# The first batch of a fused windowed attention and two-layer MLP: two single-bank tiles for layer one's first group, a vector subtraction in the first strided part, identity products on TensorE, and later turns of batch one's plain heads

## The chip, the cores and the metric

The kernel runs on one core of a Trainium2 chip. The metric is device time in microseconds (us). The engines are TensorE (PE, with its weight loads as PEld), VectorE (DVE), ScalarE (ACT), GpSimd (POOL, which here issues the loads) and SyncE (SP, which issues the stores).

## The reference

Eight batches, eight heads, 576 positions, head width 64. Heads 0 to 3 ("plain", z = 0 in the kernel) look back over 32 neighbouring positions; heads 4 to 7 ("strided", z = 1) over 32 positions that are four apart. The result is transposed to 4608 tokens of 512 features and goes through a two-layer MLP with a SiLU between.

```python
scores = scale * np.matmul(q, k.transpose(0, 1, 3, 2))
mask_plain = (rel >= 0) & (rel < window)
mask_dil = (rel >= 0) & (rel < window * dilation) & (rel % dilation == 0)
scores = np.where(masks[None, :, :, :], scores, -1000000000.0)
scores = scores - np.max(scores, axis=-1, keepdims=True)
attn = np.exp(scores)
attn = attn / (np.sum(attn, axis=-1, keepdims=True) + 1e-09)
...
h = x @ w_in                      # 4608x512 by 512x2048
g = h * (1.0 / (1.0 + np.exp(-h)))
return (g @ w_out)                # 2048x512
```

## The kernel before

Each batch goes through the same stages. `transpose` turns q and k on TensorE into head-width-major form; VectorE and ScalarE each copy half of the result out of PSUM. `scores` multiplies blocks of 32 queries with 64 keys. The row maximum is taken (`nm`, negated), the exponential follows on ScalarE (`exps`), `normal` divides by the row sum, `turned` transposes the 32x32 blocks on VectorE (`pt`), `products` multiplies with v into the PSUM tiles `x`, and `finish` copies these into `xT`. `layer1` multiplies `w_in` with `xT` into the PSUM tile `h` (SiLU on ScalarE, into `gT`), and `layer2` multiplies `gT` with `w_out` into `o`, which VectorE copies to `ob` and SyncE stores.

The schedule is written by hand: every engine works through its instructions in the order in which the program issues them. `plan_of(b)` lists, for each batch, at which unit of the MLP an attention stage of the following batches is issued. A unit is one 128-row block of layer one (units 0 to 15) or a quarter of an output tile of layer two (from 16). Batch 0 has no batch in front of it to hide its attention. So its scores are cut in two parts (`scores0`, part 0 for the first 256 positions and part 1 for the other 320), its layer one in the same two parts (`layer1_part`), and the second parts' products are issued at units -8 and -4, that is before rows 8 and 12 of layer one's first part.

PSUM has two pools: `big` with two slots of two banks each, and `ps` with four slots of one bank each. A slot is taken up again when everything that reads its former tile is done. `big` holds, in turn, the four score tiles of batch 0 (strided part 0, plain part 0, strided part 1, plain part 1) and then the `h` groups of layer one; in its first part a group is four rows of 128 by 256 columns. Only the group of rows 8 to 11 lies in two `ps` tiles.

In batch 0 there are two ways from scores to exponentials. `scaled` multiplies the negated maximum by the scale, and ScalarE then takes the exponential of each 64-wide block straight from PSUM, eight to twelve instructions with a bias and a running sum each; the score slot is held until the last of them. `shift0` adds the negated maximum on VectorE and writes the difference to SBUF; this frees the score slot, ScalarE needs a single instruction, and the row sum is then taken by a VectorE reduction in `normal`. Before the change only plain part 1 takes the second way:

```python
scores0(1, 0); scaled(1, 0)        # strided, part 0
transpose(0, 0, 1, both); transpose(0, 0, 0, both)
exps(0, 1, 0)
scores0(0, 0); scaled(0, 0); exps(0, 0, 0)
turn0(1, 0)                        # normal + turned
scores0(1, 1); scaled(1, 1); values0(1, 0); finish0(1, 0, (act, act))
exps(0, 1, 1); turn0(0, 0)
scores0(0, 1); values0(0, 0); finish0(0, 0)
shift0(0, 1); exps(0, 0, 1)
```

Lines in the profile are those of the kernel before: L243 transposes, L266 and L279 plain and strided scores, L321 the mask's product, L338 maximum, L348 `shift0`, L354 `scaled`, L418 the exponential in one instruction, L429 the exponentials by block, L438 row sum, L442 to L445 `normal`, L457 `turned`, L482 products with v, L541/L546 `finish0`, L578 `layer1_part`, L598 layer two of batch 0, L554 layer one of the later batches, L607/L608 copy and store of the output.

Of the kernel before, what the change touches and what calls it, by code (L numbers as in the profile page):

```python
# [9 lines left out]
F32 = mybir.dt.float32  # L10
# [5 lines left out]
P = 128  # L16
# [11 lines left out]
def kernel(  # L28
# [275 lines left out]
    def scores0(z, part):  # L304

        n = (2, 3)[part]
        w = width(0, z, part)
        sd = big.tile([P, 16, KB], F32, tag="big", name=f"s0_{z}_{part}")
        if z:
            sd = sd.rearrange("p (m t) c -> p m t c", m=2)  # L310
            if part:
                parts = [(sd[:, m, 0 : 2 * n], mask_b[:, 1:2].broadcast_to([W, 2 * n, KB])) for m in (0, 1)]
            else:
                pair = mask_b.rearrange("p t c -> p (t c)")[:, None, :].broadcast_to([W, 2, 2 * KB])
                parts = [(sd[:, m, 0:4].rearrange("p (e t) c -> p e (t c)", e=2), pair) for m in (0, 1)]
        elif part:
            parts = [(sd[:, o : o + x], mask_b[:, 1:2].broadcast_to([W, x, KB])) for o, x in ((0, 8), (8, 2))]
        else:
            parts = [(sd[:, 0], mask_b[:, 0]), (sd[:, 1:8], mask_b[:, 1:2].broadcast_to([W, 7, KB]))]
        for i, (t, x) in enumerate(parts):  # L320
            nc.tensor.matmul(  # L321
                t, ident4.rearrange("p h q -> p (h q)"), x,
                start=bool(z or part or i == 0), stop=True, skip_group_check=not (z or part),
            )
# [10 lines left out]
        nm = stat.tile([P, WM], F32, tag="nm", name=f"nm_0_{z}_{part}")  # L335
        raw = sd[:, :, 0 : 2 * n] if z else sd[:, 0:w]
        d = nm[:, 0:w].rearrange("p (m t) -> p m t", m=2) if z else nm[:, 0:w]
        nc.vector.tensor_reduce(out=d, in_=raw, axis=AX.X, op=ALU.max, negate=True)  # L338
        a = att(0)
        a["raw", z, part], a["nm", z, part] = raw, nm  # L340

    def shift0(z, part):

        a = att(0)
        w = width(0, z, part)
        ms = a["ms", z, part] = msp.tile([P, WM, KB], F32, tag="ms", name=f"ms_0_{z}_{part}")
        nm = a["nm", z, part][:, 0:w, None].broadcast_to([P, w, KB])
        nc.vector.tensor_tensor(ms[:, 0:w], a["raw", z, part], nm, ALU.add)  # L348
        a["shifted", z, part] = True

    def scaled(z, part):
# [59 lines left out]
    def exps(b, z, hi):  # L411
# [16 lines left out]
        for t in range(w):  # L428
# [2 lines left out]
                bias=a["nm", z, hi][:, t : t + 1], scale=k, accum_out=l[:, t : t + 1],  # L431
            )

    def normal(b, z, hi):
        a = att(b)
        w = width(b, z, hi)
        if ("shifted", z, hi) in a:
            nc.vector.tensor_reduce(  # L438
                out=a["l", z, hi][:, 0:w], in_=a["pe", z, hi][:, 0:w], axis=AX.X, op=ALU.add
            )  # L440
        r = stat.tile([P, WM], F32, tag="r", name=f"r_{b}_{z}_{hi}")
        nc.vector.tensor_scalar(r[:, 0:w], a["l", z, hi][:, 0:w], EPS, None, ALU.add)  # L442
        nc.vector.reciprocal(r[:, 0:w], r[:, 0:w])
        pn = a["pn", z, hi] = pp_.tile([P, WM, KB], F16, tag="pn", name=f"pn_{b}_{z}_{hi}")
        nc.vector.tensor_tensor(  # L445
            pn[:, 0:w], a["pe", z, hi][:, 0:w], r[:, 0:w, None].broadcast_to([P, w, KB]), ALU.mult
        )
# [70 lines left out]
                        x.rearrange("d (r i) -> d r i", r=2)[:, :, 0:CL],  # L518
                    )

    def values0(z, part):


        a = att(0)
        a["opened"] = set()
        n = (8, 10)[part] if z == 0 else (2, 3)[part]
        j0 = part * (2 if z else 8)
        x = a["x", z] = [
            ps.tile([P, WM * QB], F32, tag="ps", name=f"x_0_{z}_{part}_{hp}") for hp in (0, 1)
        ]  # L530
        for c in range(DIL if z else 1):
            products(0, z, part, c, j0, j0 + n, lambda j: (0, x, (c * n + j - j0) * QB))

# [32 lines left out]
    def layer1_part(f, part):  # L566

        xT = state[0]["xT"]
        c0, c1 = ((0, SA), (SA, S))[part]
        n, w = ((4, SA), (2, 512))[part]  # L570
        if part == 0 and f == 8:
            hs = [ps.tile([P, 2, w], F32, tag="ps", name=f"h_0_{f}_{part}_{x}") for x in (0, 1)]
        else:
            hs = [big.tile([P, n, w], F32, tag="big", name=f"h_0_{f}_{part}")]
        m = n // len(hs)
        for i in range(n):
            for c in range(MC):
                nc.tensor.matmul(  # L578
                    hs[i // m][:, i % m, 0 : c1 - c0],
                    w_in16[:, c, (f + i) * P : (f + i + 1) * P],  # L580
                    xT[:, c, c0:c1],
                    start=(c == 0),
                    stop=(c == MC - 1),
                )
# [60 lines left out]
    def plan_of(b):  # L645
        ev = {}

        def at(s, fn, *args):
            ev.setdefault(s, []).append((fn, args))

        def all_exps(b, z):
            for hi in (0, 1):
                at(16, exps, b, z, hi)

        if b == 0:

            at(-8, values0, 1, 1)
            at(-8, finish0, 1, 1, (act, act))
            at(-4, values0, 0, 1)
            at(-4, finish0, 0, 1)  # L660
            at(-4, build_mask)
            at(1, load_qk, 2)
            transposes(at, 1, 1, 2)
            at(6, scores, 1, 1)
            for hi in (0, 1):
                at(6, shift, 1, 1, hi)
            transposes(at, 1, 0, 10)
            at(14, scores, 1, 0)
            at(14, shift, 1, 0, 1)
            at(15, load_qk, 3)  # L670
            at(15, load_v, 2)
            all_exps(1, 1)
            for hi in (0, 1):
                at(20, exps, 1, 0, hi)
            later(at, 1, 1, (18, 19, 24, 25), act)
            later(at, 1, 0, (23, 24, 28, 29), act)
        elif b == 1:
            at(16, load_v, 3)
            transposes(at, 2, 0, 3)
            transposes(at, 2, 1, 10)  # L680
            transposes(at, 3, 0, 17, (dve, dve))
            at(8, scores, 2, 0)
            at(17, load_qk, 4)
            at(13, scores, 2, 1)
            all_exps(2, 0)
            all_exps(2, 1)
            at(20, scores, 3, 0)
            at(21, exps, 3, 0, 0)
            at(21, exps, 3, 0, 1)
            later(at, 2, 0, (22, 24, 27, 28))  # L690
            later(at, 2, 1, (29, 31, 33, 34))
        else:
            if b + 2 < B:
                at(16, load_v, b + 2)
            if b + 1 < B:
                if b == 2:
                    for n in (0, 1):
                        at(1 + 2 * n, transpose, 3, 1, 1 - n, both)
                later(at, b + 1, 0, (0, 0, 4, 6))
                if b + 3 < B:  # L700
                    at(16, load_qk, b + 3)
            if b + 2 < B:
                transposes(at, b + 2, 0, 13)
                at(17, scores, b + 2, 0)
# [12 lines left out]

        return plan
# [8 lines left out]
    build_mask_b()  # L727
    transpose(0, 1, 0, both)
    scores0(1, 0)
    scaled(1, 0)  # L730
    transpose(0, 0, 1, both)
    transpose(0, 0, 0, both)
    exps(0, 1, 0)
    scores0(0, 0)
    scaled(0, 0)
    exps(0, 0, 0)
    turn0(1, 0)
    scores0(1, 1)
# [62 lines left out]
```

## Time and profile before

| | us |
|---|---|
| median of 3 runs | 321.7 (321.03 to 323.43) |
| the profiled execution | 321.21 |
| its span | 319.4 |
| TensorE busy | 300.5 (94%) |
| ScalarE busy | 216.3 (68%) |
| VectorE busy | 192.5 (60%) |
| start of the first layer-one product | 21.51 |
| start of layer two of batch 0 | 45.28 |

The span runs from the first to the last instruction of the program; the 1.8 us beside it lie around the span. Busy shares are averages over stages that have different limits: TensorE is nearly idle for much of the first 21 us and nearly without a gap after it.

### The profile page before, as it was taken

How to read it: one execution, taken by the hardware profiler on the slowest of the kernel's cores; microseconds unless marked ns; L12 is line 12 of the kernel's file. 1: busy time of each engine (PE TensorE's matmuls, PEld its weight loads, DVE VectorE, ACT ScalarE, POOL GpSimd, SP SyncE). 2: the span in 40 equal slices, each digit the busy share in tenths (PEclk: the TensorE clock that was granted, in tenths of full speed). 3: DMA queues.
4: the chain of work that ended last, by engine and by line, in shares of the span. 5: the costliest groups of instructions: out<-in, count | busy, mean ns of one | idle time of the engine just before them, and what ended most of it. 6: DMA issues, size and time to landing. Idle time of an engine off the chain costs nothing.

```text
span 319.4 us, 11506 instructions
## 1 busy us (share of the span) xinstructions
PE 300.5 (94%) x5040; PEld 192.9 (60%) x5040; DVE 192.5 (60%) x360; ACT 216.3 (68%) x715; POOL 75.6 (24%) x127
## 2 busy tenths in 40 slices
PE   2669989999999999999999999999999999999995
PEld 2348644577545776467745776467745676467544
DVE  2695679616799855893587555893588542740011
ACT  2786756565999658985799458986699457726300
POOL 8825275724002800090005400060000000000000
PEclk9999999999999999999999999999999999999999
DMA  7999999995412960198016930190001100110021
GB/s 117 175 207 205 207 137 201 196 136 78 76 69 70 155 107 2 72 152 141 2 65 91 179 65 4 66 141 8 4 35 68 66 4 3 66 68 0 2 98 66
DMA packets 42081, 28.77 MB, mean 90 GB/s; under 512 B 20928, under 2 KB 37552, under 8 KB 42032
## 3 DMA queue, kind: packets, MB, share of 16 engines
q0 software_dynamic: 36704, 18.61, 44.7%
q1 hardware_dynamic: 5328, 9.44, 8.1%
q8 instruction: 39, 0.64, 0.9%
q14 instruction: 10, 0.08, 0.1%
HBM read 37.21 MB, written 9.44 MB: 146 GB/s over the span
## 4 chain that ended last, share of the span: by engine, by line
PE 80%; DVE 7%; ACT 5%; DMA 4%; issue 2%; POOL 1%; POOLq 0%; DVEq 0%
PE h L554 35%; PE o L622 30%; PE h L578 5%; PE x L482 4%; PE t L243 3%; ACT pe L429 3%; DMA n<-in_q_dram 2%; DVE pn L445 2%; DVE pt L457 2%; DMA w_in<-in_moe_w_in_dram 2%; PE s L279 1%; PE s L266 1%; DMA out_dram<-ob 1%; DVE ob L607 1%; DVE ms L297 1%
## 5 line engine op out<-in xcount | busy, mean ns | idle before, releaser
L554 PE MATMUL h<-xT,w_in 128*128 128x288 f16 x896 | 115.0, 287 | 0.2 <-DVE ob L607 0.2
L622 PE MATMUL o<-w_out,gT 128*128 128x512 f16 (+1 forms) x528 | 114.6, 373 | 0.0
L562 ACT ACTIVATE gT<-h 128x576 f16<-128x576 f32 x112 | 72.8, 650 | 59.0 <-PE h L554 58.1
L554 PEld LDWEIGHTS <-w_in 128*128 128x128 f16 x896 | 85.9, 98 | 24.1 <-issue 0.7
L622 PEld LDWEIGHTS <-gT 128*128 128x128 f16 x528 | 50.2, 98 | 54.4
L429 ACT ACTIVATE pe<-ms,nm 128x64 f32<-128x64 f32 x236 | 78.3, 334 | 0.1
L607 DVE COPY ob<-o 128x512 f32<-128x512 f32 (+1 forms) x37 | 24.8, 671 | 46.4 <-PE o L622 44.0
L429 ACT ACTIVATION_READ_ACCUMULATOR pe<-ms,nm 128x1 f32 x236 | 44.4, 188 | 0.0
L125 POOL DMA_DIRECT2D vw<-in_v_dram x32 | 18.4, 582 | 106.8 <-PE x L482 102.8
L297 DVE SCALAR_TENSOR_TENSOR ms<-s,mask 128x512 f32<-128x512 f32 x28 | 19.2, 686 | 40.3 <-PE s L279 21.6
L457 DVE STREAM_TRANSPOSE pt<-pn 128x640 f16<-128x640 f16 (+2 forms) x32 | 26.0, 812 | 1.1
L445 DVE TENSOR_TENSOR pn<-pe,r 128x640 f16<-128x640 f32 (+2 forms) x32 | 25.3, 792 | 1.1
L134 POOL DMA_DIRECT2D vw<-in_v_dram x32 | 21.2, 670 | 11.3 <-DMA w_out<-in_moe_w_out_dram 5.7
L359 DVE TENSOR_REDUCE nm<-ms 128x10 f32<-128x640 f32 (+1 forms) x28 | 22.0, 787 | 1.0
L578 PE MATMUL h<-xT,w_in 128*128 128x256 f16 (+1 forms) x128 | 18.4, 301 | 3.8 <-ACT pe L429 2.0
L482 PEld LDWEIGHTS <-vw 32*64 32x64 f16 (+1 forms) x1264 | 13.4, 107 | 8.8 <-issue 7.2
L482 PE MATMUL x<-pt,vw 32*64 32x64 f16 (+2 forms) x1264 | 15.5, 193 | 2.7 <-DVE pt L457 1.2
L578 PEld LDWEIGHTS <-w_in 128*128 128x128 f16 x128 | 12.6, 103 | 7.7 <-issue 4.2
L586 ACT ACTIVATE gT<-h 128x640 f16<-128x640 f32 (+2 forms) x13 | 9.9, 767 | 9.6 <-PE h L578 9.4
L516 DVE CAST xT<-x 128x288 f16<-128x288 f32 x24 | 16.3, 823 | 0.0
L243 PEld LDWEIGHTS <-n 64*64 64x64 f16 (+1 forms) x912 | 10.9, 105 | 6.0 <-issue 5.3
L598 PE MATMUL o<-w_out,gT 128*128 128x512 f16 x64 | 14.5, 380 | 0.0
(67 smaller groups left out, 223.4 us busy)
## 6 DMA issues: line engine op xcount, KB each, us to landing
out_dram<-ob SPq DMA_DIRECT2D x35, 256.0 KB, 2.0
n<-in_k_dram POOLq DMA_DIRECT2D x9, 288.0 KB, 5.6
n<-in_q_dram POOLq DMA_DIRECT2D x9, 288.0 KB, 6.4
vw<-in_v_dram POOLq DMA_DIRECT2D x31, 80.0 KB, 4.2
vw<-in_v_dram POOLq DMA_DIRECT2D x32, 72.0 KB, 4.0
w_in<-in_moe_w_in_dram POOLq DMA_DIRECT2D x4, 512.0 KB, 9.2
w_out<-in_moe_w_out_dram POOLq DMA_DIRECT2D x4, 512.0 KB, 11.3
n<-in_k_dram POOLq DMA_DIRECT2D x14, 144.0 KB, 7.3
```

The source lines that it names most:

```text
L134: nc.gpsimd.dma_start(out=vw[h * QB : h * QB + QB, 0:NB], in_=v[b, h].rearrange("(m p) d -> p m d", p=QB))
L297: nc.vector.scalar_tensor_tensor(out=out, in0=in0, scalar=scale, in1=in1, op0=ALU.mult, op1=ALU.add)
L359: nc.vector.tensor_reduce(out=nm[:, 0:w], in_=ms[:, 0:w], axis=AX.X, op=ALU.max, negate=True)
L429: nc.scalar.activation(pe[:, t, :], src[t], AF.Exp, bias=a["nm", z, hi][:, t : t + 1], scale=k, accum_out=l[:, t : t + 1],)
L445: nc.vector.tensor_tensor(pn[:, 0:w], a["pe", z, hi][:, 0:w], r[:, 0:w, None].broadcast_to([P, w, KB]), ALU.mult)
L457: nc.vector.transpose(a["pt"][key][:, o : o + w].rearrange("p t c -> p (t c)"), a["pn", z, hi][:, 0:w].rearrange("p t c -> p (t c)"),)
L482: nc.tensor.matmul(x[h // 2][h % 2 * D : h % 2 * D + D, col : col + wd], vws[b % 2][r, NB + kb * DIL + c if z else kb], pt[r, at : at + wd ...
L554: nc.tensor.matmul(h[:, half, 0:HS], w_in16[:, c, f * P : f * P + P], xT[:, c, half * HS : half * HS + HS], start=(c == 0), stop=(c == MC ...
L562: nc.scalar.activation(gT[:, f, s0 : s0 + S].rearrange("p (a c) -> p a c", a=2), h[:, :, 0:HS], AF.Silu)
L578: nc.tensor.matmul(hs[i // m][:, i % m, 0 : c1 - c0], w_in16[:, c, (f + i) * P : (f + i + 1) * P], xT[:, c, c0:c1], start=(c == 0), stop=( ...
L607: copy(ob, o)
L622: nc.tensor.matmul(o[:, 0, 0:m], gT[:, f, t * P : (t + 1) * P], w_out16[:, f, cols], start=(f == 0), stop=(f == NFF - 1),)
```

## The change

Four edits, all in the work of batch 0 and in the plan that is laid beside it:

- Strided part 0 of batch 0 takes the way of `shift0` in place of `scaled`. Its exponential is one instruction, issued ahead of ScalarE's copy of the plain q; its row sum (`total`) is issued on VectorE behind the two plain copies.
- `warm` issues products of the identity with itself, 256 columns each: three ahead of the products of strided part 0 (into the tile that these then overwrite), four ahead of those of plain part 0, and four ahead of layer one's first group.
- Layer one's first group of the first part (rows 0 to 3) lies in two `ps` tiles, with a SiLU each; the group of rows 8 to 11 lies in `big` with one SiLU.
- In batch 0's plan the transposes of batch 1's plain heads are issued at unit 12 (before 10), and their scores and the shift of their second half at unit 17 (before 14). Unit 17 lies behind the first four products of layer two. What is issued from unit 18 on stays.

```diff
+        nm = att(0)["nm", z, part] = stat.tile([P, WM], F32, tag="nm", name=f"nm_0_{z}_{part}")
...
-        nm = a["nm", z, part][:, 0:w, None].broadcast_to([P, w, KB])
-        nc.vector.tensor_tensor(ms[:, 0:w], a["raw", z, part], nm, ALU.add)
+        nm, o = a["nm", z, part][:, 0:w], ms[:, 0:w]
+        if z:
+            o = o.rearrange("p (m t) c -> p m t c", m=2)
+            nm = nm.rearrange("p (m t) -> p m t", m=2)[:, :, :, None].broadcast_to([P, 2, w // 2, KB])
+        else:
+            nm = nm[:, :, None].broadcast_to([P, w, KB])
+        nc.vector.tensor_tensor(o, a["raw", z, part], nm, ALU.add)
...
+    def total(b, z, hi):
+        a = att(b)
+        w = width(b, z, hi)
+        nc.vector.tensor_reduce(
+            out=a["l", z, hi][:, 0:w], in_=a["pe", z, hi][:, 0:w], axis=AX.X, op=ALU.add
+        )
+        a["summed", z, hi] = True
...
+    def warm(t, n):
+
+        for _ in range(n):
+            nc.tensor.matmul(
+                t[:, 0:SA], ident, ident[:, None, :].broadcast_to([P, SA // P, P]),
+                start=True, stop=True, skip_group_check=True,
+            )
...
+        warm(x[0], idle)          # values0, ahead of its products
...
-        if part == 0 and f == 8:
+        if part == 0 and f == 0:
             hs = [ps.tile([P, 2, w], F32, tag="ps", name=f"h_0_{f}_{part}_{x}") for x in (0, 1)]
+            warm(hs[0].rearrange("p n w -> p (n w)"), 4)
...
-            transposes(at, 1, 0, 10)
-            at(14, scores, 1, 0)
-            at(14, shift, 1, 0, 1)
+            transposes(at, 1, 0, 12)
+            at(17, scores, 1, 0)
+            at(17, shift, 1, 0, 1)
...
     scores0(1, 0)
-    scaled(1, 0)
+    shift0(1, 0)
     transpose(0, 0, 1, both)
+    exps(0, 1, 0)
     transpose(0, 0, 0, both)
-    exps(0, 1, 0)
+    total(0, 1, 0)
     scores0(0, 0)
...
-    values0(1, 0)
+    values0(1, 0, 3)
...
-    values0(0, 0)
+    values0(0, 0, 4)
```

Against the kernel before, TensorE has eleven more products with their weight loads ahead of layer one; VectorE has one instruction more; ScalarE has the exponential of strided part 0 once in place of eight times, and copies batch 1's plain k and q behind the SiLU of rows 10 and 11 and no longer ahead of it.

More of the change, by code (lines that the diff above doesn't have):

```diff
@@ L334, in scores0 @@
                     score(0, h, 8 * part + j, sd[:, j], False)
-        nm = stat.tile([P, WM], F32, tag="nm", name=f"nm_0_{z}_{part}")
+        nm = att(0)["nm", z, part] = stat.tile([P, WM], F32, tag="nm", name=f"nm_0_{z}_{part}")
         raw = sd[:, :, 0 : 2 * n] if z else sd[:, 0:w]
@@ L339, in scores0 @@
         a = att(0)
-        a["raw", z, part], a["nm", z, part] = raw, nm
+        a["raw", z, part] = raw
     def shift0(z, part):
@@ L436, in normal @@
         w = width(b, z, hi)
[L437 to L440, printed above, removed]
+        if ("shifted", z, hi) in a and ("summed", z, hi) not in a:
+            total(b, z, hi)
         r = stat.tile([P, WM], F32, tag="r", name=f"r_{b}_{z}_{hi}")
@@ L519, in finish, with values0 @@
                     )
-    def values0(z, part):
+    def warm(t, n):
[4 more added lines that the diff above has]
+            )
+    def values0(z, part, idle=0):
         a = att(0)
```

## The prediction

> **What bounds the kernel now.** I read the page's totals first, then what TensorE waits for, then the first 30 us in order of time.
>
> ```profile
> span 319.4 us, 11506 instructions
> PE 300.5 (94%) x5040; PEld 192.9 (60%) x5040; DVE 192.5 (60%) x360; ACT 216.3 (68%) x715; POOL 75.6 (24%) x127
> PE t L227 <- DMA n<-in_k_dram: 5.5, 1, 5.5
> PE h L578 <- ACT pe L429: 2.0, 1, 2.0
> PE h L578 <- issue: 1.8, 1, 1.8
> PE t L243 <- issue: 0.6, 1, 0.6
> ```
>
> TensorE is busy for all but 18.9 us, and 5.5 of these are the first load. Of its other waits the longest ends with ScalarE's exponentials by block (L429), which hold the score slots; the next is put down to "issue", which no semaphore explains. So time won ahead of layer one shows in the end, if no later wait takes it back. The change works on the stretch that follows (the timeline: start, duration, engine, line):
>
> ```profile
> 9.23 0.69 DVE L338 TENSOR_REDUCE nm<-s 128x8 f32<-128x512 f32 x1 [0.90 <-PE s L279]
> 10.03 0.75 DVE L247 COPY kT<-t 128x576 f16<-128x576 f16 x1
> 11.02 0.76 DVE L247 COPY qT<-t 128x576 f16<-128x576 f16 x1 [0.23 <-PE t L243]
> 11.59 0.32 ACT L429 ACTIVATE pe<-s,nm 128x64 f32<-128x64 f32 x1
> 11.83 0.61 PE L266 MATMUL s<-kT,qT 64*32 64x64 f16 x32 [0.31 <-DVE qT L247]
> 12.50 0.69 DVE L338 TENSOR_REDUCE nm<-s 128x8 f32<-128x512 f32 x1 [0.72 <-PE s L266]
> 13.92 0.36 ACT L429 ACTIVATE pe<-s,nm 128x64 f32<-128x64 f32 x1
> 14.12 0.80 PE L321 MATMUL s<-mask_b,ident 32*128 32x384 bf16 x2 [1.68 <-ACT pe L429]
> 15.27 0.71 DVE L457 STREAM_TRANSPOSE pt<-pn 128x512 f16<-128x512 f16 x1
> 16.13 0.61 PE L482 MATMUL x<-pt,vw 32*64 32x64 f16 x32 [0.67 <-DMA w_in<-in_moe_w_in_dram]
> 16.67 0.71 PE L321 MATMUL s<-mask_b,ident 32*128 32x512 bf16 x2
> 16.78 1.29 ACT L541 CAST xT<-x 128x256 f16<-128x256 f32 x2 [0.34 <-PE x L482]
> 18.10 0.71 DVE L457 STREAM_TRANSPOSE pt<-pn 128x512 f16<-128x512 f16 x1
> 18.87 0.61 PE L482 MATMUL x<-pt,vw 32*64 32x64 f16 x32 [0.83 <-DVE pt L457]
> 19.52 0.76 DVE L546 CAST xT<-x 128x256 f16<-128x256 f32 x2
> 21.27 0.81 ACT L418 ACTIVATE pe<-ms 128x640 f32<-128x640 f32 x1
> 21.51 4.98 PE L578 MATMUL h<-xT,w_in 128*128 128x256 f16 x32 [2.02 <-ACT pe L429]
> 25.98 0.84 DVE L457 STREAM_TRANSPOSE pt<-pn 128x640 f16<-128x640 f16 x1
> 27.04 1.92 PE L578 MATMUL h<-xT,w_in 128*128 128x256 f16 x16
> 28.89 0.70 PE L482 MATMUL x<-pt,vw 32*64 32x32 f16 x44
> ```
>
> The reader sees two things at 21.51. Both halves of plain xT have been there since 20.28, yet layer one waits for ScalarE's twelve exponentials, whose slot its group takes. And its first 32 products take 4.98 us where 16 of the same form take 1.92 later: TensorE starts slowly. The windows view shows how far (a stretch, then TensorE's busy time and count in it):
>
> ```profile
> 21.60:24.20 2.60, 2.60 (x13) 1.84 (x13) 1.00 1.23 208
> ```
>
> Up to 24.2 a product comes each 0.2 us (0.21, since one of the 13 began earlier). The 16 at 27.04 come each 0.11, with the last one's own length at their end, and 13 of 0.21 and 19 of 0.11 make the 4.98. So the clock doubled near 24.2, though the granted clock in that row (1.00) does not show it.
>
> **Strided part 0.** Removed: eight exponentials, 2.33 us of ScalarE (11.59 to 13.92), and a scaling of 0.17 on VectorE. Added: one exponential of 128x512, which I take at 0.65 (0.81 is the row for 640 columns; by width it would be 0.65), a subtraction of 0.69 and a reduction of 0.69 on VectorE (512 columns, as L338's). The subtraction runs from 9.95 to 10.64 in front of the plain copies: kT goes from 10.03 to 10.56, qT from 11.02 to 11.24, for it waited 0.23 on TensorE before. Plain scores so start at 12.05 and no longer at 11.83, the maximum at 12.72 (the reduction for the sum ends at 12.6, just ahead), and ScalarE starts on the plain exponentials at 13.70 instead of 13.92. Of 2.33 us saved on ScalarE the path gets 0.2, since the work behind it comes later.
>
> What gains more is VectorE: the strided turn waits for no accumulator. Its transpose ends at 15.40, not 15.98, and the strided products run at 15.55, not 16.13. Strided part 1's scores, in a slot that is free at 10.64, run at 12.55, not 14.12. These scores end by 14.0. The next ones need the plain exponentials' slot, free near 16.2 (13.70 and eight blocks of 0.29, with the last sum's read-out), so they start at 16.28 for 16.67. ScalarE's copies start at 16.26 for 16.78; the twelve exponentials behind them, whose end lets TensorE go at 21.51 now, end as much earlier, near 20.95. The plain transpose ends at 18.23 for 18.81, its products start at 18.36 for 18.87, VectorE's copies at 19.03 for 19.52.
>
> **Identity products.** Each takes 0.21 us while slow. Three fit between 13.9 and 15.55. Four from 17.45 end at 18.30, when the plain transpose is ready. Four from 18.8 end at 19.62, while the xT copies run. All are covered; without that cover the last two groups would cost 0.85 us each.
>
> **Two single banks.** The `ps` tiles are free when ScalarE's copies end, at 17.55. Layer one starts as soon as xT is there, at 19.65, the second product at 19.85: 1.8 us earlier. Its second group takes the slot that the exponentials free at 20.95, reached later than that. The plain second part of attention takes up the two `ps` tiles, so it needs their SiLUs. These stand right behind the exponential that now begins at 21.27, and have until 26.4. The extra SiLU costs ScalarE a start, under the 0.65 of a whole such instruction, in that same slack.
>
> **The clock.** It doubled 2.7 us after the first layer-one product. In the changed kernel TensorE is occupied nearly without a gap from 16.3 on, with full-size products from 17.45. If it again takes some 2.7 to 3.4 us of those, the clock comes at 20.2 to 20.9; if the identity products did nothing, at about 24.2 as now. I take 20.9. The Trainium skill ("TensorE: Matmul & The Clock Gate", Part 1) has free-running windows of 3.4 us; by them the clock would come at 24.2 - 3.4 = 20.8, or a window later. The trace agrees with the doubling.
>
> With 20.9, 32 products from 19.65 end near 23.7 (26.4 now), and the strided second part (under 0.7, as its plain sister at 28.89) and 16 more products (1.8) near 26.1. There VectorE takes over: its last transpose, now until 26.83, follows the twelve exponentials and ends at 26.31, so the plain second part runs at 26.40 for 28.89. **Head: 2.5 us.** With the clock at 24.2 it would be 1.1.
>
> **Units 12 and 17.** Now the rows behind it:
>
> ```profile
> 38.47 0.83 PE L243 MATMUL t<-ident,n 64*64 64x64 f16 x72
> 39.23 0.44 PE L578 MATMUL h<-xT,w_in 128*128 128x320 f16 x2
> 41.47 2.07 PE L578 MATMUL h<-xT,w_in 128*128 128x320 f16 x14 [1.80 <-issue]
> 43.47 0.70 PE L266 MATMUL s<-kT,qT 64*32 64x64 f16 x64
> 45.28 8.02 PE L598 MATMUL o<-w_out,gT 128*128 128x512 f16 x36
> 53.23 0.34 PE L482 MATMUL x<-pt,vw 32*64 32x64 f16 x20
> 54.23 0.71 PE L482 MATMUL x<-pt,vw 32*64 32x64 f16 x60 [0.67 <-DVE r L442]
> 48.26 0.82 DVE L438 TENSOR_REDUCE l<-pe 128x10 f32<-128x640 f32 x1 [0.37 <-ACT pe L418]
> 62.68 0.69 DVE L607 COPY ob<-o 128x512 f32<-128x512 f32 x1 [0.62 <-DMA out_dram<-ob]
> q8 instruction: 39, 0.64, 0.9%
> q8 instruction: 1, 0.02, 2.7%
> 35.75:39.50 3.75, 3.75 (x139) 2.71 (x137) 3.23 (x6) 2.13 (x4) 0.66 (x1) 1.00 1.25 209
> 41.40:83.60 42.20, 40.67 (x767) 26.16 (x768) 27.25 (x47) 27.18 (x53) 21.51 (x35) 1.00 1.07 149
> ```
>
> The wait at 39.5 I read as one for code. The queue for instructions moves 39 blocks for TensorE's 10080 instructions, 258 each; one of them moves between 39.2 and 41.4 (second q8 line, the DMA view of that stretch). Between the two "issue" waits lie 767 products and 768 loads, six times 256: both stand at a block's start. So a block begins two products behind the transposes. The block before it began 256 instructions earlier, near 35.75, inside batch 1's strided scores (the window to 39.50 counts 276 with those in flight at its start). If crossing that border asks for the next block, it was at hand 5.7 us later, at 41.47. The 22 added instructions move the borders back, the second one into the transposes, and one more group of eight products (1.09, at 0.136 each by the row at 41.47) stands in between. TensorE needs the block 3.75 + 1.09 - 0.35 = 4.5 us after it asks: the wait falls from 1.96 to 1.2 us, **0.75 gained**. Bounds: none left, or as long as before. The Trainium skill ("Runtime: NRT & Kernel Launch", Instruction fetch mechanics) calls such a crossing mostly hidden; these rows disagree, and by it the wait would be gone, the first rival below.
>
> The move puts two things ahead of batch 1's plain scores: the group of rows 14 and 15 (1.09) and four products of layer two (0.88, a ninth of the 8.02 for 36), 1.97 us. They start at 43.47 - 2.5 - 0.75 + 1.97 = 42.2. This matters, because from these scores to the strided products of unit 24 the chain of waits lies on VectorE without a pause (43.47 to 54.23, but for 0.37 on ScalarE, which is early now). So the products' second part starts at 42.2 + 10.76 - 0.37 = 52.6, for 54.23: 1.63 earlier. TensorE is there at 50.0 (42.2 and 9.76, as from 43.47 to 53.23, less the 1.97 of work that now lies ahead) and stands 2.3 us, some of it behind the 20 products that are ready, instead of 0.7: half of what was won ends here. From there both chains keep their distance. The stores of batch 0 start earlier into loads that keep their time; the fourth copy waits for the first store (0.62). I take 0.2 lost, from 0 (the store takes as long as now) to 1.6 (it lands when it does now).
>
> **Sum.** 2.5 + 0.75 - 1.97 + 0.37 - 0.2 = 1.45 us off the profiled 321.21: **319.8**, which is 1.9 under the median of 321.7.
>
> **Rivals.** (a) *The code wait goes away*: 1.2 more, 318.6; if stores cost nothing either, 318.4. For it: the border's place is inferred. Against it: both waits stand at borders. (b) *The postponed scores set the end, and slower*: VectorE's chain is paid for 1.97 us of delay minus 0.37, whatever the head wins, so from a gain ahead of it under 1.6 us the kernel loses. With the clock at 24.2 (1.1) and a code wait as now, that is 0.5 lost, 321.7; a code wait 1 us longer makes 322.7. For it: small products alone, busy much of 14 to 18, did not raise the clock. Against it: the identity products are full-size. (c) *The head's gain is lost at the stores*: 321.2, if each lands when it does now. Against it: the loads around 58 leave as much as those around 60.
>
> **How the numbers follow.** The forecast, 319.1 to 320.8, has 0.55; (a) 0.2; (b) 0.13; (c) 0.12. The range is 317.8 to 322.0: (a) with the best bounds and the milder half of (b). Faster by over 1% (a bound of 3.2 us, about what this kernel's measurement tells) needs under 318.5: about half of (a) and a tail of a head better than I see, 0.18. Slower by over 1% would need (b) with more besides: 0.06. The rest, 0.76, lies within 1%.
>
> **What would show it.** Right: strided part 1's scores near 12.6, layer one's first product near 19.7 with products of 0.11 apart from about 21, plain second part near 26.4, a wait of 1 to 1.5 us inside batch 1's plain transposes, and one of over 2 us at the strided products near 50 to 52.6. Wrong: the clock still slow at 23, no wait at unit 24, or a code wait of 2 us or more.

## The result, and the profile after

The changed kernel takes 320.5 us (median of 22 runs, 319.11 to 321.8); the kernel before, run beside it, 323.63 us (321.03 to 325.06). The ratio is 0.9909, interval 0.9889 to 0.9929: about 0.9% faster. The forecast was 319.8 us, a gain of 1.9 us against the median then known. The time came out near the forecast, but not all terms of the sum did, and errors of both signs cancelled.

The profiled execution of the changed kernel took 321.8 us. Two rows of its page, the span and the granted clock in 40 slices:

```profile
span 320.0 us, 11511 instructions
...
PEclk9999979999999999999999999999999999999999
```

The span is 0.6 us *longer* than the 319.4 of the first profile, although the medians differ by 3.1 us the other way. So the two profiles must be compared stretch by stretch, and the digit 7 in the clock row, at about 40 us, is the first thing to ask about. In the head, strided part 1's scores run at 12.69 (forecast 12.55) and the strided products at 15.54 (15.55). Then:

```profile
19.88 3.70 PE L599 MATMUL h<-xT,w_in 128*128 128x256 f16 x32
...
26.54 0.53 PE L493 MATMUL x<-pt,vw 32*64 32x32 f16 x44 [0.36 <-DVE pt L468]
```

Layer one (L599, L578 before) starts at 19.88 and its 32 products take 3.70 us where they took 4.98. With a product each 0.11 us and 0.2 at the end, 3.70 is the fast clock from the first product on. (In what follows, each product at the slow clock adds 0.1 us to 3.70 and takes 0.21; so 5.65 us is 19 or 20 slow ones and a clock that rose some 4 us after the start.) The plain second part runs at 26.54, 2.35 us earlier than before. Then, behind it:

```profile
37.03 0.64 PE L243 MATMUL t<-ident,n 64*64 64x64 f16 x56
39.93 0.32 PE L243 MATMUL t<-ident,n 64*64 64x64 f16 x16 [2.25 <-issue]
40.18 4.02 PE L599 MATMUL h<-xT,w_in 128*128 128x320 f16 x16
45.00 0.70 PE L266 MATMUL s<-kT,qT 64*32 64x64 f16 x64
...
55.40 0.71 PE L493 MATMUL x<-pt,vw 32*64 32x64 f16 x60 [2.35 <-DVE r L453]
64.72 2.12 PE L574 MATMUL h<-xT,w_in 128*128 128x288 f16 x16 [0.28 <-DVE ob L628]
83.71 0.90 PE L243 MATMUL t<-ident,n 64*64 64x64 f16 x72
```

The code wait stands inside batch 1's plain transposes, as forecast, but is 2.25 us by this row, where 1.2 was forecast. The 16 products of layer one behind it take 4.02 us; the same form takes 2.35 where no such wait precedes it. The windows view of two stretches shows why (the clock is the third number from the end, ahead of the DMA share and GB/s):

```profile
36.87:40.28 3.41, 1.16 (x75) 0.85 (x74) 2.34 (x4) 1.23 (x2) 0.98 (x2) 1.00 1.25 204
40.28:43.69 3.41, 3.41 (x14) 1.90 (x14) 0.76 (x1) 1.34 (x2) 1.98 (x3) 0.50 1.82 166
```

TensorE was busy for 1.16 of 3.41 us, and then worked for 3.41 us at half clock: about 1.7 us lost. Batch 1's plain scores so start at 45.00 and not at 42.2. The wait at unit 24 is there (2.35 us, forecast 2.3). At 64.72 the changed kernel is 1.30 us *behind* the first profile's 63.42. It wins 0.69 of this back at 83.7, where the kernel before had its second "issue" wait, in batch 3's plain transposes, and the changed kernel has none:

```profile
63.42 2.12 PE L554 MATMUL h<-xT,w_in 128*128 128x288 f16 x16 [0.15 <-DVE ob L607]
...
83.62 0.38 PE L243 MATMUL t<-ident,n 64*64 64x64 f16 x23 [0.61 <-issue]
83.93 2.77 PE L622 MATMUL o<-w_out,gT 128*128 128x512 f16 x12
```

(This is the kernel before; behind the wait layer two goes on at 83.93, in the changed kernel at 84.54.) From there to the end the distance stays at 0.6 us.

### The profile page after: what moved, and what is told of

Its sections match the earlier page's. It is cut to its first block, busy times and chain, and to the rows that moved or that the text cites. A ratio compares the mean times of both kernels' runs of the same rounds, so it can differ in the third digit from the quotient of the medians.

```text
span 320.0 us, 11511 instructions
## 1 busy us (share of the span) xinstructions
PE 303.0 (95%) x5051; PEld 194.0 (61%) x5051; DVE 194.1 (61%) x361; ACT 214.5 (67%) x700; POOL 75.9 (24%) x127
## 4 chain that ended last, share of the span: by engine, by line
PE 79%; DVE 11%; ACT 5%; DMA 3%; issue 2%; POOL 0%; DVEq 0%; POOLq 0%
PE h L574 35%; PE o L643 30%; PE h L599 4%; ACT pe L434 4%; PE t L243 3%; PE x L493 3%; DVE pn L456 2%; DVE pt L468 2%; PE s L279 2%; DMA n<-in_q_dram 2%; PE s L266 1%; DMA out_dram<-ob 1%; DVE ob L628 1%; DVE ms L297 1%; DVE l L442 1%
## 5 line engine op out<-in xcount | busy, mean ns | idle before, releaser
L599 PE MATMUL h<-xT,w_in 128*128 128x256 f16 (+1 forms) x128 | 18.4, 304 | 0.0
L243 PE MATMUL t<-ident,n 64*64 64x64 f16 (+1 forms) x912 | 13.0, 193 | 2.8 <-issue 2.3
L599 PEld LDWEIGHTS <-w_in 128*128 128x128 f16 x128 | 12.8, 103 | 4.1
```

The source lines that it names most:

```text
L243: nc.tensor.transpose(dst, w, ident[r, r])
L599: nc.tensor.matmul(hs[i // m][:, i % m, 0 : c1 - c0], w_in16[:, c, (f + i) * P : (f + i + 1) * P], xT[:, c, c0:c1], start=(c == 0), stop=( ...
```

## The experiments

Ratios are to the kernel before on the same chip. What comes back in most of them are two waits for code ("issue", at the plain transposes of batch 1 near 39 us and of batch 3 near 84), and a halved clock behind a long wait. Each of the kernels below has one profile, of one execution; its landmarks are those of that execution, and only the ratios rest on several runs.

**The kernel before, profiled again** (no edit, one execution). Why is the first profile 2.4 us under this kernel's later median?

> The kernel before, unchanged, for a second profile. Theory (the first profile of it fell on a lucky position of the clock's windows; most executions lose more): a time near 323 us, with the doubled clock later than 24.3 us, or taken away again for 3.4 us after the wait near 40 us. Rival (the first profile is typical of the kernel, and the later runs are slower for another reason, spread over the span): the same clock as in the first profile, and a longer time elsewhere.

The time was 324.32 us; the kernel's other runs there had a median of 324.27. Its rows:

```profile
28.51 0.70 PE L482 MATMUL x<-pt,vw 32*64 32x32 f16 x44
...
63.41 2.12 PE L554 MATMUL h<-xT,w_in 128*128 128x288 f16 x16 [0.65 <-DVE ob L607]
85.06 0.38 PE L243 MATMUL t<-ident,n 64*64 64x64 f16 x23 [1.82 <-issue]
85.37 4.45 PE L622 MATMUL o<-w_out,gT 128*128 128x512 f16 x12
85.40:88.80 3.40, 3.40 (x15) 1.17 (x10) 1.42 (x2) 3.40 (x22) 0.00 (x0) 0.50 0.02 5
```

The plain second part runs 0.38 us earlier than in the first profile (28.89), and at 63.41 this execution stands where the first stood (63.42). The loss that was expected behind the wait near 40 us comes behind the other one: its second code wait is 1.82 us and not 0.61, and behind it 12 products of layer two take 4.45 us for 2.77, at half clock: 1.2 and 1.7 us, nearly all of the 3.1 by which its span is longer (322.5 us). So the profile on which the forecast was built was one of this kernel's quick executions. Against this one the changed kernel is 1.31 us behind at 64.72; it is 0.83 ahead once the second code wait is passed (84.54 for 85.37), and another 1.68 ahead behind the slow products: 2.5 us, the whole difference of the spans. **In this pair the gain comes from a place at which no edit was aimed, and what the head won is more than used up by 65 us.**

**Units back** (all of the change but the later units).

```diff
-            transposes(at, 1, 0, 12)
-            at(17, scores, 1, 0)
-            at(17, shift, 1, 0, 1)
+            transposes(at, 1, 0, 10)
+            at(14, scores, 1, 0)
+            at(14, shift, 1, 0, 1)
```

> The changed kernel, but batch 1's plain transposes, scores and shift back at units 10, 14 and 14. Theory (the later units cost time, because VectorE's chain from the plain scores to the strided products of unit 24 starts later): scores near 42 to 44 instead of 45.0, the second strided products 1 to 2 us earlier than 55.4, time 1 to 2 us under the changed kernel, although the code wait inside the transposes gets longer (one group of 8 products less in front of it: 3.3 us instead of 2.3). Rival (the later units are what gains, because they shorten the code wait): 1 us or more slower than the changed kernel.

319.33 us (6 runs), ratio 0.987 (0.9829 to 0.991): the lowest ratio of all the kernels run. Its profile, the timeline and two windows, laid in steps of 3.41 us from where its clock rose (21.10 us in the trace):

```profile
38.84 0.26 PE L243 MATMUL t<-ident,n 64*64 64x64 f16 x8 [2.14 <-issue]
39.02 2.35 PE L599 MATMUL h<-xT,w_in 128*128 128x320 f16 x16
52.06 0.71 PE L493 MATMUL x<-pt,vw 32*64 32x64 f16 x60 [0.67 <-DVE r L453]
61.51 2.12 PE L574 MATMUL h<-xT,w_in 128*128 128x288 f16 x16 [0.40 <-DVE ob L628]
34.75:38.17 3.42, 1.95 (x74) 1.31 (x73) 3.39 (x6) 1.94 (x3) 0.66 (x1) 1.00 1.24 205
38.17:41.58 3.41, 2.74 (x62) 1.91 (x62) 1.72 (x3) 1.51 (x3) 0.66 (x1) 1.00 1.31 199
```

The wait at unit 24 is 0.67 us and no longer 2.35, as the prediction's working has it. The code wait is as long as in the changed kernel, not the microsecond longer that was expected, yet the 16 products behind it take 2.35 us: here the wait is split between two windows, busy 1.95 and 2.74 us, and the clock stays. At 61.51 this kernel is 1.9 us ahead of the kernel before (63.41), as much as its plain second part (26.57) is ahead of that of the same profile (28.51): the head's gain is whole. By the medians (319.33 and 320.5) the later units would cost about 1.2 us, but the two intervals overlap, and a second pair of kernels that differ in the units alone shows no cost: 0.9891 with units 12 and 17 and 0.9891 with units 10 and 14, both with strided part 0 by block (the first and the last of the parts below). Part of the 1.2 us can be the clock: four of these six runs had a mean granted clock of 1.0, and eight of the changed kernel's 22 had 0.999 or 1.0; those alone have medians of 319.1 and 319.6. So the longer wait at unit 24 is shown, and a cost in the time is not.

**No identity products** (`warm` issues none).

```diff
-        for _ in range(n):
+        for _ in range(0):
```

> The changed kernel without the eleven identity products. Theory (they bring the doubled clock one window of 3.4 us earlier): the first layer-one products 0.21 us apart until 22 to 24 us, plain second part of batch 0 near 27.5 to 28 instead of 26.5, time 1 to 1.5 us over the changed kernel. Rival (the clock would rise as early from the real products alone, now closer together): same time within 0.3 us.

323.33 us (12 runs), ratio 0.999 (0.9956 to 1.0025): without them nothing is left of the gain, a loss of 2.6 us by the ratios where 1 to 1.5 were expected.

```profile
19.54 5.65 PE L599 MATMUL h<-xT,w_in 128*128 128x256 f16 x32 [0.61 <-DVE xT L566]
27.59 0.53 PE L493 MATMUL x<-pt,vw 32*64 32x32 f16 x44
...
54.34 5.30 PE L619 MATMUL o<-w_out,gT 128*128 128x512 f16 x16
66.23 2.12 PE L574 MATMUL h<-xT,w_in 128*128 128x288 f16 x16 [2.05 <-DVE ob L628]
87.20 0.37 PE L243 MATMUL t<-ident,n 64*64 64x64 f16 x22 [1.38 <-issue]
```

The head loses 1.05 us of the 1.4 that the prediction gave for a late clock (the clock rises about 4 us later, plain second part at 27.59 for 26.54). The other losses lie far behind it: 16 products of layer two take 5.30 us for 3.63 behind the wait at unit 24, the store makes TensorE wait for 2.05 us, and batch 3's code wait is back at 1.38. Removing 11 products also removes 22 instructions, which moves every border behind them.

**The same 22 instructions elsewhere** (no identity products, but eleven small ones at the start of the program, where TensorE waits for its first load).

```diff
-        for _ in range(n):
+        for _ in range(0):
...
+    pads = [big.tile([P, 16, KB], F32, tag="big", name=f"pad_{i}") for i in (0, 1)]
+    for i in range(11):
+        r = slice(i % 4 * W, i % 4 * W + W)
+        nc.tensor.matmul(
+            pads[0][r, 0, 0:W], ident[r, 0:W], ident[r, 0:W],
+            start=True, stop=True, skip_group_check=True,
+        )
```

> The changed kernel with its eleven identity products replaced by the 11 small products at the start, so that from layer one on the code stands where it stands in the changed kernel, without products that keep TensorE busy ahead of layer one. Theory (the identity products gain by both, the clock and the border): 321.5 to 322.5 us, between the changed kernel (320.5) and the one without identity products (323.3). Rivals: the clock is all (323.3), or the border is all (320.5).

321.06 us (12 runs), ratio 0.9923 (0.9889 to 0.9956).

```profile
20.12 4.84 PE L599 MATMUL h<-xT,w_in 128*128 128x256 f16 x32 [0.61 <-DVE xT L566]
39.93 0.32 PE L243 MATMUL t<-ident,n 64*64 64x64 f16 x17 [1.27 <-issue]
83.61 0.47 PE L243 MATMUL t<-ident,n 64*64 64x64 f16 x33 [0.52 <-issue]
```

From the ratio 0.999 without these instructions to 0.9909 of the change, the way is 0.0081, or 2.6 us; 0.0067 of it, 2.2 us, come with 22 instructions that stand nowhere near layer one. Some 0.4 us is left for what the identity products do where they stand, and the intervals do not separate that from nothing. So most of the gain comes with 22 more instructions ahead of batch 1, at either place (the intervals with and without them, 0.9889 to 0.9956 and 0.9956 to 1.0025, just touch). That they must keep TensorE busy in front of layer one is not shown, and warming as the main reason falls.

**The kernel before with the same eleven products at its start.** If the position of the code were all, it would gain.

```diff
...
+    for i in range(11):
...
```

> The kernel before with 11 products of 32x32 identities (22 instructions, as many as the identity products are) at its very start, under the wait for the first load; nothing else is changed. Theory (part of the gain is no work at all: 22 more instructions move the border of a code block inside batch 3's plain transposes, so that the second code wait, 0.8 to 2.0 us near 83 us, nearly goes, and with it a halved clock behind it): second code wait under 0.7 us, time 0.8 to 1.5 us under the kernel before. Rival (the second code wait hangs on the loads of the moment, not on the border): no difference beyond 0.3 us.

323.9 us (12 runs), ratio 0.9996 (0.9968 to 1.0025): a miss.

```profile
41.39 0.36 PE L243 MATMUL t<-ident,n 64*64 64x64 f16 x9 [2.31 <-issue]
41.68 3.76 PE L578 MATMUL h<-xT,w_in 128*128 128x320 f16 x16
84.72 1.05 PE L243 MATMUL t<-ident,n 64*64 64x64 f16 x72
```

Batch 3's transposes (84.72) have no wait, as expected. But the first code wait has grown to 2.31 us and halves the clock behind it (3.76 for 2.35). So in this kernel the moved borders bring nothing, and the 2.2 us above are not to be had by position alone either.

**Forty more products** (units back, and forty of the same small products, 80 instructions, at the start). If the first code wait is a border, it must come 40 of the transposes' products earlier: behind 24, and no longer behind 64.

```diff
...
+    for i in range(40):
...
```

> The kernel with units 10 and 14 and 40 products of 32x32 identities (80 instructions) ahead of the first transposes, where TensorE waits for the first load. Theory (a block of 256 instructions ends inside batch 1's plain transposes): the border moves 40 products forward, so the wait falls behind about 24 of the 72 products instead of 64, and it shortens from 2.1 to about 1 us, as the block is asked for earlier; time 0.5 to 1.5 us under the kernel with units 10 and 14. Rival (the wait belongs to this place in the work): it stays behind 64 products.

```profile
20.27 0.40 PE L493 MATMUL x<-pt,vw 32*64 32x64 f16 x16 [1.13 <-issue]
39.15 0.38 PE L243 MATMUL t<-ident,n 64*64 64x64 f16 x24
39.91 0.62 PE L243 MATMUL t<-ident,n 64*64 64x64 f16 x48 [0.38 <-issue]
45.28 0.24 PE L266 MATMUL ss<-kT,qT 64*32 64x64 f16 x8 [1.46 <-issue]
```

It stands behind the 24th. That this wait belongs to the border of a block of code, as the prediction inferred, is shown. The time was 324.98 us (12 runs, ratio 1.0027, 0.9999 to 1.0055), over 5 us more than units back where a gain of 0.5 to 1.5 was expected: other borders now fall into groups of small products and wait there, 1.13 and 1.46 us, and in this execution 22 of layer one's first 32 products were slow (5.91 us from 21.43 on).

**Fewer loads** (is it the loads that delay the block of code?). `hold` makes GpSimd wait for a SiLU before it issues the loads behind it. This kernel leaves out three quarters of `w_out`: all of layer two multiplies with the first quarter, so its output is not the reference's, and its time serves this question alone.

```diff
-    for c in range(4):
-        load_w_out(c)
-    load_v(1)
+    load_w_out(0)
...
-            at(1, load_qk, 2)
+            at(13, hold)
+            at(15, load_v, 1)
+            at(15, load_qk, 2)
...
+    def hold():
+        nc.gpsimd.tensor_copy(scratch, gT[:, 11, SA : SA + 8])
...
-                        o, gT[:, f, t * P : (t + 1) * P], w_out16[:, f, :],
+                        o, gT[:, f, t * P : (t + 1) * P], w_out16[:, f % 4, :],
```

> The changed kernel with less to load around 33 to 40 us: only the first quarter of w_out is loaded (all of layer two uses it), and the loads of batch 1's v and batch 2's q and k wait for the SiLU of row 11 of layer one's second part. Theory (the wait inside batch 1's plain transposes is one for code, long because its block queues behind other loads): the block's transfer starts 1 us and not 4.5 us after the border is crossed, so the wait falls from 2.3 us to under 0.5, no halved clock behind it, time 1.5 to 3 us under the changed kernel. Rival (the wait is no transfer, or does not hang on the loads): it stays at 2 us.

320.19 us (4 runs), ratio 0.9892 (0.9852 to 0.9933).

```profile
20.23 5.16 PE L597 MATMUL h<-xT,w_in 128*128 128x256 f16 x32
...
27.80 0.53 PE L491 MATMUL x<-pt,vw 32*64 32x32 f16 x44
...
38.29 0.83 PE L241 MATMUL t<-ident,n 64*64 64x64 f16 x72
53.12 5.31 PE L617 MATMUL o<-w_out,gT 128*128 128x512 f16 x16
```

Batch 1's transposes (L241 here) run unbroken: without the loads there is no first code wait. The time hardly moves, where 1.5 to 3 us were expected. In the profiled execution, the slowest of the four (322.26), the clock rose late (5.16 us for the first 32), was halved behind unit 24 (5.31 us for 3.63), and a store made TensorE wait for 1.64.

**The loads held back** (units back; the last three quarters of `w_out`, `v` of batch 1 and q, k of batch 2 loaded from unit 8 on; all are used).

```diff
-            at(1, load_qk, 2)
+            at(8, hold)
+            for c in (1, 2, 3):
+                at(8, load_w_out, c)
+            at(8, load_v, 1)
+            at(8, load_qk, 2)
...
+        nc.gpsimd.tensor_copy(scratch, gT[:, 7, SA : SA + 8])
```

> The changed kernel with units 10 and 14, and with the loads of the last three quarters of w_out, of batch 1's v and of batch 2's q and k held back until the SiLU of rows 6 and 7 of layer one's second part is done. Theory (the wait for code inside batch 1's transposes is long because its block queues behind these loads): the wait falls from 2.3 us to under 0.5, no halved clock there, time 1.5 to 2.5 us under the kernel with units 10 and 14 (319.3), if no later load comes too late. Rival (the loads are late then, w_out's second quarter at the fifth product of layer two): a wait on a load near 46 us, no gain.

322.31 us (12 runs), ratio 0.9956 (0.9921 to 0.999): 3 us slower than units back, where a gain was expected.

```profile
36.14 0.83 PE L241 MATMUL t<-ident,n 64*64 64x64 f16 x72
64.00 3.71 PE L572 MATMUL h<-xT,w_in 128*128 128x288 f16 x16 [3.88 <-DVE ob L626]
64.30:67.70 3.40, 3.40 (x19) 1.91 (x21) 0.00 (x0) 0.65 (x1) 1.34 (x2) 0.50 1.24 228
```

The first code wait is gone again. But the loads, pushed later, now run beside batch 0's stores: between 54 and 64 us a store lands 6.8 us after its issue (median of four), where units back has 3.5. VectorE's copy waits, TensorE stands for 3.88 us and then works at half clock. This is the wait of the prediction's rival (c), provoked.

**Parts alone.** *Strided part 0 by block* (`scaled` as before, the rest of the change kept):

```diff
-    shift0(1, 0)
+    scaled(1, 0)
     transpose(0, 0, 1, both)
-    exps(0, 1, 0)
     transpose(0, 0, 0, both)
-    total(0, 1, 0)
+    exps(0, 1, 0)
```

> The changed kernel, but strided part 0 with eight exponentials by block from PSUM as before. Theory (this edit gives about half a microsecond on the path, by VectorE's turn): first layer-one product near 20.4 instead of 19.9, last transpose of batch 0 half a microsecond later, time 0.3 to 0.8 us over the changed kernel. Rival (the slot held by the eight exponentials matters more, 1.6 us at strided part 1's scores): 1.5 us or more over it.

320.09 us (6 runs), ratio 0.9891 (0.9849 to 0.9933), against 0.9909 with the subtraction: this edit brings nothing that shows in the time, where 0.3 to 0.8 us were expected. Layer one starts at 20.14 for 19.88, and the first code wait in this profile is 1.29 us.

*One tile* (rows 0 to 3 in `big`; four identity products in two `ps` tiles that nothing reads):

```diff
         if part == 0 and f == 0:
+            for x in (0, 1):
+                warm(ps.tile([P, 512], F32, tag="ps", name=f"warm_{x}"), 2)
+        if part == 0 and f == 8:
             hs = [ps.tile([P, 2, w], F32, tag="ps", name=f"h_0_{f}_{part}_{x}") for x in (0, 1)]
-            warm(hs[0].rearrange("p n w -> p (n w)"), 4)
```

> The changed kernel, but layer one's first group in one two-bank tile and the group of rows 8 to 11 in two single-bank tiles, as before; the four identity products ahead of it write to throw-away tiles. Theory (two single banks start layer one a microsecond earlier, but VectorE's last transpose takes most of it at the plain second part): first product near 21.0 instead of 19.9, plain second part near 26.9 instead of 26.5, time 0.3 to 0.5 us over the changed kernel. Rival (the early start is worth its full 1.1 us): 1 us over it.

323.02 us (12 runs), ratio 0.9986 (0.9957 to 1.0015): no gain, and a loss of 2.5 us against the changed kernel where 0.3 to 0.5 were expected. Its timeline:

```profile
20.89 6.16 PE L601 MATMUL h<-xT,w_in 128*128 128x256 f16 x32 [0.79 <-ACT pe L434]
29.46 0.70 PE L493 MATMUL x<-pt,vw 32*64 32x32 f16 x44
```

Layer one waits for the exponentials' slot again, until 20.89; some 25 of the 32 products are slow, and the plain second part comes at 29.46. Without the two banks the other edits gain nothing. That the gap in front of layer one is what delays the clock is a reading of this one execution.

*Banks and identity products alone* (`scaled` in strided part 0, units 10 and 14; its two diffs stand above):

> Of the four edits only the two single banks and the identity products; strided part 0 and units 10 and 14 as before. Theory (these two bring the gain, the subtraction brings nothing that lasts, the later units cost): 319.0 to 320.0 us, as fast as the changed kernel or 0.5 to 1 us faster. Rival (the four edits need each other): over 321 us.

320.82 us (6 runs), ratio 0.9891 (0.9859 to 0.9923). In its profile the clock rose late in spite of the identity products (4.95 us for layer one's first 32, plain second part at 27.68), and the first code wait is 2.11 us, with the halving behind it:

```profile
39.92 0.28 PE L243 MATMUL t<-ident,n 64*64 64x64 f16 x8 [2.11 <-issue]
40.13 3.95 PE L599 MATMUL h<-xT,w_in 128*128 128x320 f16 x16
```

Two of the four edits already have the change's ratio.

## Why the prediction was right, and where it was wrong

The forecast time, 319.8, lies 0.7 us from the measured 320.5, and that is partly luck. The sum stood on a quick execution of the kernel before, and three things that it left out or could not know (a halved clock, a second border and a late transfer) pull in both directions.

- **Head, 2.5 us: right in this execution.** Layer one 19.88 (forecast 19.65), the clock up by its first product (20.9 would have done), plain second part 26.54 (26.40): 2.35 us against the first profile, 1.97 against the second. Each landmark on the way lies within 0.25 us. That the clock rose so early is not assured: with the same head, the kernel with fewer loads had some 15 slow products and its plain second part at 27.80, a head of 1.1 us, which is the prediction's figure for a late clock. The kernels without identity products (27.59, or 27.36 with the eleven at the start) are no later than that, so what these products give by the clock is not shown. Without the two banks the plain second part came at 29.46. Strided part 0's subtraction brought layer one 0.26 us forward, and leaving it out changes nothing that the timing can tell.
- **Code wait, "falls from 1.96 to 1.2 us": right in place and, but for this execution, in size.** The sum rests on "at hand 5.7 us later", the time from crossing one border to having the block behind the next. Counted back 128 products with their weight loads from where TensorE goes on, the rows are, first for the changed kernel, then for strided part 0 by block, whose border lies at the same product:

```profile
33.19:39.93 6.74, 4.49 (x141) 3.25 (x128) 5.46 (x9) 3.18 (x5) 2.00 (x3) 1.00 1.24 206
33.57:39.39 5.82, 4.53 (x153) 3.29 (x128) 5.23 (x9) 3.22 (x5) 1.43 (x3) 1.00 1.24 207
```

The same count gives 5.6 to 5.9 us in nine profiles, both of the kernel before among them (5.0 with forty more products), and 6.74 in the changed kernel's alone: there the block's transfer began 4.5 us behind the border, in the nine 3.3 to 3.7. So with the units at 12 the wait was 1.29, 1.28, 1.27 and 1.06 us in four kernels, as forecast, and 2.25 in this one; with the units at 10 and the border inside the transposes, where the extra group of products is not in front of it, it was 2.14, 2.11 and 2.31. Why one transfer began a microsecond late stays open. The prediction had named a code wait of 2 us or more as a sign that it is wrong, and in this execution the sign was there.
- **The halved clock: not foreseen.** In this execution it took 1.7 us, which is most of the 2.8 us by which batch 1's scores missed 42.2; the rest is the code wait's extra 1.05 us. The sum 2.5 + 0.75 - 1.97 had no term for what a long wait does to the products behind it. With it the profile adds up: 2.35 us of head, less 0.3 for the code wait, 1.7 for the clock, 1.6 for the units and 0.1 for the stores, leaves the changed kernel 1.35 us behind the first profile, and at 64.72 it is 1.30 behind.
- **Units, -1.97 + 0.37: right at unit 24, not shown in the time.** The wait there is 2.35 us (2.3 forecast), and without the later units 0.67. Of two pairs that differ in the units alone, one shows a cost of about 1.2 us with overlapping intervals and the other none.
- **Stores, -0.2: about right.** The first one costs 0.28 us where it cost 0.15 in the first profile (0.65 in the second).
- **The base: not foreseen.** The sum was made against 321.21 us, an execution with a short second code wait and no halved clock, quicker than 21 of the 22 runs of the kernel before; their median is 323.63. The changed kernel takes the forecast 319.8 without the halving: its runs whose mean clock was 0.999 or 1.0 lie at 319.1 to 320.7.
- **The border in batch 3's transposes: not foreseen.** The prediction moved the borders by 22 instructions at one place and did not ask what the same move does at the other place which it had named. There the wait goes (1.8 or 0.6 us to none), and in the pair with the second profile this wait and the halved clock behind it are the whole gain.

Of the rivals, (a) had the right event at the wrong border; (b) describes what the units do, and code wait and clock took the head's gain below its 1.6 us: at 64.7 us the changed kernel was behind, as (b) has it, and won only by the second border; (c) did not come, though the held loads show that such a wait can.

What stays open: one profile per kernel shows one execution, and where the windows of the clock and the loads stand against the waits differs from run to run. Of the changed kernel's 22 runs, 14 had a mean granted clock of 0.995 to 0.998; 0.995 is what one window of 3.4 us at half clock makes of 320 us. The clock alone does not explain the gain: the changed kernel's runs at 0.999 or 1.0 have a median of 319.6 us and those at 0.995 one of 321.1, while the kernel before, in the runs beside the experiments, has 322.9 (28 runs) and 325.1 (29 runs at 0.995 or less). The gain is 3 us or more in both groups. How it divides between head and borders is known from pairs of profiles, not from medians.

## What to carry to other kernels

Before a small gain is put down to the edit, profile the unchanged kernel a second time, and compare landmarks stretch by stretch: here the whole difference of one pair lay near 85 us, some 40 us behind the last changed instruction. When an edit adds or removes instructions on an engine with long code, list every group of small instructions that a block border falls into before and after, while loads are heavy. A wait of 2 us on TensorE can cost nearly twice its length, by the products behind it.

## What the runs showed of the hardware

**A long wait halves TensorE's clock, if it falls into one window.** Windows busy 1.16 of 3.41 us (the changed kernel), or 1.58 of 3.40 (the kernel before, second profile), were followed by 3.4 us at half clock; one busy 1.95, which held only the first 1.5 us of such a wait, was not. The rows of the changed kernel and of units back stand above; this is the second profile of the kernel before:

```profile
82.00:85.40 3.40, 1.58 (x77) 0.89 (x76) 1.56 (x3) 3.37 (x11) 0.00 (x0) 1.00 0.47 83
```

So the border lies somewhere between 46% and 57% in these runs. In the traces a halving lasts 3.41 us and begins a whole number of such windows behind the clock's rise: six in the changed kernel (19.80 to 40.28), 18 in the second profile of the kernel before (23.96 to 85.40). The Trainium skill ("TensorE: Matmul & The Clock Gate", Part 1) gives a free-running window of 3.4 us, with which the halved stretches agree, and lets the clock fall after an idle window of that length; here windows that were a third to nearly half busy did it, and the measurement decides.

**The clock's rise at the start is not settled by busy time alone.** Windows of 3.41 us that end where the clock did or did not rise, first the changed kernel and then the one with fewer loads:

```profile
16.39:19.80 3.41, 3.41 (x82) 2.04 (x82) 3.12 (x8) 3.41 (x20) 0.89 (x2) 1.00 1.24 207
```

```profile
16.49:19.90 3.41, 3.27 (x81) 1.96 (x81) 3.18 (x9) 3.41 (x20) 1.24 (x2) 1.00 1.24 206
```

Nearly the same work: the clock rose after the first and not after the second, where it took one window more. With banks and identity products alone even a window that was busy for all of its 3.41 us (16.14 to 19.55) was followed by slow products up to about 23. What the criterion is stays open.

**Code can arrive late.** A block of 256 instructions moves once per border, and in the stretch before these waits the 16 DMA engines were busy without a pause. In the DMA view of the changed kernel TensorE's queue (q8) moves no block from 33 to 37.5 us and one from 37.5 to 39, and TensorE goes on at 39.93 (the view's head and that queue's line):

```profile
DMA packets 297, 0.31 MB, mean 210 GB/s; under 512 B 5, under 2 KB 296, under 8 KB 296
q8 instruction: 1, 0.02, 4.1%
```

The block is one packet among 297. With the loads taken away, the wait was gone. The Trainium skill ("Runtime: NRT & Kernel Launch", Instruction fetch mechanics) calls a crossing mostly hidden; most borders here are (39 blocks move in the profile before, and two show such a wait), and those in groups of small products under load cost up to 2.3 us.
